# Head groups of a decode attention kernel in a hardware loop, with four fixed cache slots

## The chip, the cores and the metric

One core of one Trainium2 chip runs the kernel. The metric is the device time of one execution in microseconds, as the median of several runs. A second figure, the span, comes from the hardware profile of one run: from the first to the last instruction.

The profile names the engines: PE does matmuls and PEld loads their weights, DVE is the vector engine, ACT the scalar engine, POOL the one called GpSimd, and SP (SPq for its sequencer) is SyncE, which here issues the large DMA transfers. The granted clock is PE's clock as a share of full speed. A semaphore is a counter by which one engine waits for another. PSUM is the memory that matmuls write to.

## The reference

One decode step for two sequences (B = 2): attention with 32 query heads on 8 key/value heads over a cache of 32768 positions, a small MLP beside it, and a gate.

```python
def reference(A_x, A_k_cache, A_v_cache, A_wq, A_wo, B_x, B_w1, B_w2, B_w3, B_w4):
    xn = layernorm(A_x)                                   # [2, 1, 512]
    q  = (xn @ wq)                                        # 32 heads of 128
    p  = softmax(q @ k_cache^T * 128 ** -0.5)             # k, v: [2, 8, 32768, 128]
    s  = (p @ v_cache) @ wo
    # S is 1, so the shifted mix of the MLP's first half is zero and x1 = xn
    g  = silu(xn + gelu(layernorm(xn) @ w3) @ w4)
    return A_x + s * g
```

The caches are 268 MB in bfloat16. Everything else is 12 MB.

## The kernel before

There are 16 head groups (b, g), each with two tiles of K and two of V, 4 MB apiece. All 32 (K, V) pairs are written out by Python. Five slots of 4 MB rotate among the weights, the K tiles and the V tiles. SyncE issues all large loads in the order of the program. The code is shortened.

```python
    for r in range(NR):                       # emit_k: 8 blocks of one K tile
        nc.vector.transpose(T, kt[block r])   # DVE
        4 x nc.tensor.matmul(sc, lhsT=z[...], rhs=T[...])
    nc.scalar.activation(ep, sc, Exp, accum_out=rs)
    nc.vector.transpose(pt, ep)
    ...                                       # emit_v: sums of rs, then
    32 x nc.tensor.matmul(o, lhsT=pt[...], rhs=vt[...])     # four column tiles
    # after the second V tile of a group: ob <- o, oT, divide by the sum, onx
    ...
    for n in range(NW + 1):                   # 32 pairs, written out
        if n + 2 < NW: k_tiles[n + 2] = load_cache(A_k_cache, ...)
        if 0 < n + 1 < NW: v_tiles[n + 1] = load_cache(A_v_cache, ...)
        if n == NW - 1: load wo in five pieces
        if n < NW: eps[n] = emit_k(n)
        if n == 1: emit_mlp()                 # between two K tiles
        if n > 0: emit_v(n - 1, eps.pop(n - 1))
    for r in range(RW):                       # 32 rows x 4 column tiles: 128 matmuls
        for n in range(NQ):
            nc.tensor.matmul(s_ps[32*n:32*n+B], lhsT=oX[:, r, :], rhs=wo3[:, r, n*QW:(n+1)*QW], ...)
    # out = s_ps * g4 + x4, two DVE operations, then two small stores
```

The softmax here doesn't subtract the row's maximum and nothing guards it: scores larger than these inputs give would overflow.

## Time and profile before

| | before |
|---|---|
| time, median | 662.1 us |
| span | 660.5 us |
| bytes through SyncE's queue | 280.5 MB |
| GB/s from 100 to 640 us | 432 |
| last input byte landed | 655.3 us |
| from there to the span's end | 5.2 us |

The times of last bytes, here and below, are read from the trace's DMA packets of 1 KB and more.

From the page of the kernel before. The first line gives each engine's busy time. The rows of digits are tenths of busy time in 40 slices. The q1 row gives packets, MB and share of the 16 DMA engines. The DMA 75% row belongs to the chain of work that ended last. The last row ends with the time from issue to landing.

```profile
PE 408.5 (62%) x2590; PEld 173.7 (26%) x2622; DVE 344.9 (52%) x422; ACT 50.1 (8%) x152; POOL 6.9 (1%) x20
...
DMA  9999999999999999999999999999999999999995
...
q1 hardware_dynamic: 10232, 280.50, 98.6%
q8 instruction: 20, 0.33, 0.2%
...
DMA 75%; PE 15%; DVE 6%; issue 2%; ACT 0%; SPq 0%; DVEq 0%; ACTq 0%
...
k<-in_A_k_cache_dram SPq DMA_DIRECT2D x32, 4096.0 KB, 43.8
```

The DMA never rests. PE and DVE are far from full. A K load lands 44 us after its issue, so about 4.5 tiles of 9.7 us stand in the queue.

The windows view of the kernel before (a stretch in us, its length, busy time of PE, PEld, DVE, ACT and POOL, granted clock, DMA share, GB/s). It counts a packet in the stretch in which it starts, so a short stretch can show a share over 1.00:

```profile
20.00:22.00 2.00, 0.00 (x0) 0.00 (x0) 0.00 (x0) 1.12 (x1) 0.00 (x0) 1.00 0.65 279
22.00:26.00 4.00, 0.39 (x1) 0.11 (x2) 1.69 (x2) 0.00 (x0) 0.00 (x0) 1.00 1.17 501
...
100.00:640.00 540.00, 344.07 (x1929) 140.89 (x1960) 292.56 (x336) 37.15 (x118) 0.00 (x0) 0.77 1.00 432
```

At the end of the kernel before, the timeline shows the output matmuls in two parts. The second part waits for the last pieces of wo.

```profile
651.57 1.49 PE L402 MATMUL s_ps<-wo,oX 128*2 128x128 bf16 x64 [0.29 <-DVE oX L372]
...
654.07 2.09 PE L402 MATMUL s_ps<-wo,oX 128*2 128x128 bf16 x64 [1.01 <-DMA wo<-in_A_wo_dram]
...
656.21 0.29 DVE L410 TENSOR_TENSOR sg<-s_ps,g 98x128 f32<-98x128 f32 x1 [4.70 <-PE s_ps L402]
```

### The profile page before, as it was taken

The page shows a single profiled execution, that of the slowest core. Times are in us where ns is not written, and L with a number is a line of the kernel's source. Part 1 is how long each engine was busy: PE and PEld are TensorE (multiplying, and loading weights), DVE is VectorE, ACT ScalarE, POOL GpSimd, SP SyncE. Part 2 cuts the span into 40 slices and gives each one's busy share as a digit, 9 for nine tenths or more (in the row PEclk, how much of TensorE's full clock was granted, in tenths as well). Part 3 has the DMA queues.
Part 4 walks back from the last instruction along what each step waited for, and adds up shares of the span by engine and source line. Part 5 has one row for each costly group of instructions (what it writes and reads, how often), then busy time and mean ns, then how long its engine had stood idle before and what let it go on. Part 6 is the DMA issues. An engine that isn't in the chain of part 4 may idle for free.

```text
span 660.5 us, 6182 instructions
## 1 busy us (share of the span) xinstructions
PE 408.5 (62%) x2590; PEld 173.7 (26%) x2622; DVE 344.9 (52%) x422; ACT 50.1 (8%) x152; POOL 6.9 (1%) x20
## 2 busy tenths in 40 slices
PE   2485667565566756466776456777645776556564
PEld 2242223222222322223222122322212232222223
DVE  4563456555445655445656444565644466554450
ACT  1111100000000000000000000000000000000000
POOL 3000000000000000000000000000000000000000
PEclk9986897676888767678777777877777787767886
DMA  9999999999999999999999999999999999999995
GB/s 381 418 437 442 416 442 435 425 442 429 430 439 422 439 440 421 440 433 426 443 429 426 443 426 433 434 429 438 433 428 439 426 435 440 425 435 438 427 428 210
DMA packets 10527, 280.89 MB, mean 425 GB/s; under 512 B 1402, under 2 KB 1540, under 8 KB 1668
## 3 DMA queue, kind: packets, MB, share of 16 engines
q1 hardware_dynamic: 10232, 280.50, 98.6%
q8 instruction: 20, 0.33, 0.2%
q0 software_dynamic: 256, 0.01, 0.0%
q14 instruction: 7, 0.06, 0.0%
q10 hardware_dynamic: 12, 0.00, 0.0%
HBM read 280.50 MB, written 0.00 MB: 425 GB/s over the span
## 4 chain that ended last, share of the span: by engine, by line
DMA 75%; PE 15%; DVE 6%; issue 2%; ACT 0%; SPq 0%; DVEq 0%; ACTq 0%
DMA k<-in_A_k_cache_dram 69%; PE sc L309 11%; DMA wo<-in_A_wo_dram 6%; DVE T L301 6%; PE o L341 3%; DVE pt L320 1%; ACT ep L318 0%; PE S L337 0%; SPq L390 0%; DVE sm L336 0%; SPq L97 0%; PE s_ps L402 0%; DVE sg L410 0%; DVE out L412 0%; DVEq L301 0%
## 5 line engine op out<-in xcount | busy, mean ns | idle before, releaser
L309 PE MATMUL sc<-T,z 128*128 128x512 bf16 x992 | 295.2, 457 | 190.6 <-DVE T L301 183.3
L301 DVE STREAM_TRANSPOSE T<-k 128x1024 int32<-128x1024 int32 x256 | 292.2, 1208 | 173.4 <-DMA k<-in_A_k_cache_dram 173.4
L309 PEld LDWEIGHTS <-z 128*128 128x128 bf16 x1024 | 114.5, 112 | 370.5 <-issue 289.9
L341 PE MATMUL o<-v,pt 128*16 128x512 bf16 x1024 | 75.5, 447 | 4.9 <-DMA v<-in_A_v_cache_dram 4.9
L320 DVE STREAM_TRANSPOSE pt<-ep 128x512 bf16<-128x512 bf16 x32 | 22.8, 711 | 79.2 <-ACT ep L318 79.2
L318 ACT ACTIVATE ep<-sc 128x512 bf16<-128x512 f32 x32 | 19.1, 597 | 533.4 <-PE sc L309 533.4
L341 PEld LDWEIGHTS <-pt 128*16 128x16 bf16 x1024 | 25.6, 99 | 42.2 <-issue 25.3
L337 PE MATMUL S<-sm,ones_f 128*128 128x4 f32 x64 | 12.0, 258 | 24.8 <-DVE sm L336 24.8
L353 PE MATMUL oT<-sel_o,ob 128*128 128x4 f32 x128 | 16.9, 255 | 11.1 <-ACT ob L350 11.1
L353 PEld LDWEIGHTS oT<-sel_o,ob 128*128 128x128 f32 x128 | 15.5, 191 | 19.4 <-ACT ob L350 19.4
L337 PEld LDWEIGHTS S<-sm,ones_f 128*128 128x128 f32 x64 | 9.7, 190 | 32.6 <-DVE sm L336 32.6
L332 DVE MEMSET o<- 128x512 f32 x16 | 7.8, 485 | 13.4 <-ACT ob L350 12.3
L285 ACT COPY z<-qr 32x16 bf16<-32x16 bf16 x64 | 12.6, 197 | 11.5 <-DVE qr L232 10.8
L360 DVE TENSOR_TENSOR on<-oT,rec 128x4 f32<-128x4 f32 x16 | 2.6, 163 | 20.2 <-PE oT L353 20.2
L350 ACT COPY ob<-o 128x512 f32<-128x512 f32 x16 | 9.4, 586 | 26.2 <-PE o L341 26.2
L358 DVE RECIPROCAL rec<-S 128x4 f32<-128x4 f32 x16 | 2.9, 183 | 7.3 <-PE S L337 7.2
L318 ACT ACTIVATION_READ_ACCUMULATOR ep<-sc 128x1 f32 x32 | 6.3, 198 | 0.2
L214 PE MATMUL qT_ps<-xT,wq 128*128 128x2 bf16 x128 | 3.6, 165 | 4.5 <-DMA wq<-in_A_wq_dram 4.5
L336 DVE TENSOR_SCALAR sm<-sel_h,rs 128x4 f32<-128x4 f32 x32 | 6.1, 190 | 0.0
L214 PEld LDWEIGHTS <-wq 128*128 128x128 bf16 x128 | 3.5, 104 | 4.6 <-DMA wq<-in_A_wq_dram 4.6
L197 PE MATMUL treg<-ident,xn_bf 2*128 2x2 bf16 x4 | 0.3, 173 | 6.8 <-DVE xn_bf L189 6.8
L402 PE MATMUL s_ps<-wo,oX 128*2 128x128 bf16 x128 | 3.5, 286 | 1.3 <-DMA wo<-in_A_wo_dram 1.0
(63 smaller groups left out, 42.3 us busy)
## 6 DMA issues: line engine op xcount, KB each, us to landing
k<-in_A_k_cache_dram SPq DMA_DIRECT2D x32, 4096.0 KB, 43.8
v<-in_A_v_cache_dram SPq DMA_DIRECT2D x32, 4096.0 KB, 39.3
wq<-in_A_wq_dram SPq DMA_DIRECT2D x1, 4096.0 KB
w<-in_B_w_dram SPq DMA_DIRECT2D x2, 1792.0 KB, 37.7
wo<-in_A_wo_dram SPq DMA_DIRECT2D x1, 2048.0 KB, 34.3
wo<-in_A_wo_dram SPq DMA_DIRECT2D x1, 1536.0 KB, 37.7
wo<-in_A_wo_dram SPq DMA_DIRECT2D x1, 384.0 KB, 38.3
wo<-in_A_wo_dram SPq DMA_DIRECT2D x1, 119.0 KB
```

The lines of the kernel that those rows point to most:

```text
L214: nc.tensor.matmul(qT_ps[:, h * B:(h + 1) * B], lhsT=wq3[:, k, h * Dh:(h + 1) * Dh], rhs=xT[:, k, :], start=(k == 0), stop=(k == DK - 1),)
L285: nc.scalar.copy(out=z[32 * j:32 * j + 32, :, :, c:c + rep], in_=qr[32 * j:32 * j + 32, :, :, b, g * rep:(g + 1) * rep],)
L301: nc.vector.transpose(out=T[:, :].rearrange("p (b t k) -> p t b k", b=NB, t=RT), in_=kt[:, r * W:(r + 1) * W].rearrange("p (t b k) -> p t ...
L309: nc.tensor.matmul(sc[:, :], lhsT=z[:, nb, e, zc:zc + 128], rhs=Tb[:, nb, :, e], start=(r == 0 and nb == 0 and e == 0), stop=(r == NR - 1 ...
L318: nc.scalar.activation(out=ep[:, :], in_=sc[:, :], func=ACT.Exp, scale=inv_sqrt_dh, accum_out=rs[:, :])
L320: nc.vector.transpose(out=pt[:, :, :].rearrange("p r (t h) -> p t r h", h=rep), in_=ep[:, :].rearrange("p (t r h) -> p t r h", r=NR, h=rep),)
L332: nc.vector.memset(state["o"][:, :], 0.0)
L336: nc.vector.tensor_scalar_mul(out=sm[:, :], in0=sel_h[:, :], scalar1=rs[:, 0:1])
L337: nc.tensor.matmul(S[:, :], lhsT=ones_f[:, :], rhs=sm[:, :], start=(i == 0), stop=(i == NPART - 1))
L341: nc.tensor.matmul(o[32 * j:32 * j + VT * rep, :], lhsT=pt[:, r, a * VT * rep:(a + 1) * VT * rep], rhs=vt[:, u * VT:(u + 1) * VT, :].rearr ...
L350: nc.scalar.copy(out=ob[:, :], in_=o[:, :])
L353: nc.tensor.matmul(oT[:, :], lhsT=ob[:, t * Dh:(t + 1) * Dh], rhs=sel_o[:, t, :], start=(t == 0), stop=(t == VT - 1),)
```

## The change

The intent is a much smaller program: one head group is a turn of a hardware loop. Semaphores are not reset between turns. Instead every wait on what the loop itself counts compares with a register that grows by one turn's worth of increments. Fixed slots k0, k1, v0, v1 replace the rotation, and a fifth slot holds wo. wq first uses v0 and the MLP's weights use v1, so q and the whole MLP are done before the loop. The output stage stands in an `If` in the last turn.

```diff
-    slots = ctx.enter_context(tc.tile_pool(name="slots", bufs=SLOTS))
+    slots = ctx.enter_context(tc.tile_pool(name="slots", bufs=1))
-    wq_t = slot("wq")
+    wq_t = slot("v0", "wq")
-    k_tiles[0] = load_cache(A_k_cache, *work[0], "k0")
-    k_tiles[1] = load_cache(A_k_cache, *work[1], "k1")
-    w34 = slot("w34")
+    w34 = slot("v1", "w34")
 ...
-    v_tiles[0] = load_cache(A_v_cache, *work[0], "v0")
 ...                                  # q, then
+    emit_mlp()
 ...
-    for n in range(NW + 1):
-        ...                           # loads ahead, emit_k(n), emit_v(n - 1)
+    with tc.For_i(0, B * Hkv, 1, iteration_sync="reg_based") as n:
+        ks = [load_cache(A_k_cache, n, i, f"k{i}") for i in range(NPART)]
+        vs = [load_cache(A_v_cache, n, i, f"v{i}") for i in range(NPART)]
+        emit_z(n)
+        eps = [emit_k(k) for k in ks]
+        S = f_ps.tile([128, rep], F32, tag="S", name="S")
+        for i in range(NPART):
+            emit_v(vs[i], *eps[i], S, i)
+        emit_out(n, S)
+        with tc.If(n == B * Hkv - 1):
+            emit_end()                # loads wo, 128 output matmuls, result
```

## The prediction

> **What bounds the kernel now.** The page of the profile says 280.50 MB through the SyncE queue, the DMA row at 9 in 39 of 40 slices, and 425 GB/s over the span. The windows view gives 432 to 433 GB/s and a DMA share of 1.00 from 80 to 640 us. The Trainium skill ("DMA: Bandwidth & Descriptors", the bandwidth table at its head) puts the fabric's ceiling at 435 GB/s; this trace agrees within 1%. So about 649 us are transfer; the last wo piece lands at 655.9, and 4.6 us of tail follow. The chain of waits is 75% DMA. PE is 62% busy, DVE 52%.
>
> **What the change does.** The bytes stay the same. Five rotating slots become four fixed ones (K0, K1, V0, V1) plus one that only wo uses, so fewer loads are in flight; now a K load lands 44 us after its issue, i.e. about 4.5 tiles of 9.7 us are queued. Does the queue ever run dry?
>
> Timeline of one turn, an estimate from durations of this trace. K0 lands at T, then K1, V0, V1 at steps of 9.7 (T+9.7, T+19.4, T+29.1). Eight transposes of one K tile take 9.1 us; exp, transposition of ep and the row sum some 3.5; 32 V matmuls 1.9 to 3.5. The slots come free at about T+9 (K0), T+19 (K1), T+25 (V0; its matmuls now stand behind both K tiles) and T+31 to 33 (V1). The queue reaches their next loads at T+29, T+39, T+48.5 and T+58. So each load is issued about 20 us or more early; two to three tiles stay queued (landing falls to some 27 to 35 us). Transfers should stay back to back.
>
> Added per turn, all hidden in that slack: register arithmetic before nearly every DVE transpose, a compare at the If, a back edge, and a wait of SyncE, in the turns without the output stage, until this turn's K0 and K1 have landed (T+9.7; K0 frees then anyway). The Trainium skill ("Runtime: NRT & Kernel Launch", Instruction fetch mechanics) says a taken branch out of the fetched pages stalls for a fetch; no trace here shows its size. Over some 6 us on DVE would delay the next K0's transposes; over 15 us per turn would empty the queue.
>
> Start: wq and w34 go first (19 us), then K0 and K1 without a wait, V0 after q, V1 after the MLP (about 28 us; the queue holds work to 39). No gap. End: wo is issued about when the last V1 is, and lands last as before; the tail is the same 4.6 us, plus the loop's exit (compare, drain, one more all-engine barrier, perhaps a fetch): 1 to 4 us, the only part on the critical path.
>
> **Prediction.** 664 us, range 660.5 to 671. Faster by over 2%: 1%; within 2%: 92%; slower by over 2%: 7%.
>
> **What would show it.** DMA row still 9 nearly everywhere, about 432 GB/s in mid-span windows, 38.8 us between successive K0 landings; K landing time down to 25 to 35 us; last wo piece within 2 us of 656; a longer gap from out's issue to the end. Wrong if a window shows GB/s dipping once per turn (stall at the back edge or shallow queue), if ISA instructions stretch the DVE chain from 9.1 us a tile to over 13, or wo starts after a gap.
>
> **What would make it wrong.** Branch stalls that add up along K0 to the output; engines of the DMA drifting apart so far that the shallower queue starves the fast ones; a late issue of wo.

## More of the kernel before

SyncE's DMA issues at the start, from the timeline (start, duration, line, what):

```profile
0.74 0.42 SPq L97 DMA_DIRECT2D wq<-in_A_wq_dram  x1
1.22 0.88 SPq L87 DMA_DIRECT2D k<-in_A_k_cache_dram  x2
2.14 0.61 SPq L112 DMA_DIRECT2D w<-in_B_w_dram  x1
2.79 0.49 SPq L113 DMA_DIRECT2D w<-in_B_w_dram  x1
3.33 0.50 SPq L87 DMA_DIRECT2D v<-in_A_v_cache_dram  x1
```

All five slots are asked for within 4 us.

## The result

The changed kernel takes 670.5 us median (669.95 to 672.05, four runs) against 662.1. The ratio is 1.0129, with a 95% interval of 1.0111 to 1.0146. Ratios here are the mean time of one kernel's fast runs over the mean of the other's in the same rounds, so they are not quite the ratio of the medians quoted. Where two of my kernels are compared across calls, I multiply their ratios to the kernel before by 662 us.

The page of the changed kernel, the same rows:

```profile
PE 421.3 (63%) x2622; PEld 178.4 (27%) x2622; DVE 335.3 (50%) x407; ACT 71.3 (11%) x167; POOL 6.2 (1%) x19
...
DMA  8699999999999999999999999999999999999993
...
q1 hardware_dynamic: 10232, 280.50, 97.5%
q8 instruction: 3, 0.05, 0.0%
...
v<-in_A_v_cache_dram SPq DMA_DIRECT2D x32, 4096.0 KB, 32.9
```

The DMA row has one weak slice, the second, and then stays at 9. No turn of the loop shows a dip. A V tile lands some 33 us after its issue (39.3 before), as a shorter queue would have it. The page gives no such figure for K here; in the timeline a K0 issued at 320.70 us is first transposed at 348.87, so it had landed within 28.2 us. The windows view agrees:

```profile
20.00:22.00 2.00, 1.48 (x25) 1.40 (x24) 0.42 (x3) 0.00 (x0) 0.00 (x0) 1.00 0.38 152
22.00:26.00 4.00, 1.66 (x56) 1.37 (x56) 1.33 (x7) 1.82 (x3) 0.00 (x0) 1.00 0.02 4
...
100.00:640.00 540.00, 351.84 (x1946) 141.66 (x1945) 282.95 (x321) 58.24 (x140) 0.00 (x0) 0.79 1.00 434
```

From 22 to 26 us the DMA moved nothing to speak of. From 100 us on the loop streams at 434 GB/s, a little more than before. SyncE's issues (timeline) and one row of SyncE's waits (who waited for whom: total, times, longest) give the reason:

```profile
1.66 0.50 SPq L109 DMA_DIRECT2D w<-in_B_w_dram  x1
25.67 0.96 SPq L86 DMA_DIRECT2D k<-in_A_k_cache_dram  x2
26.96 1.01 SPq L86 DMA_DIRECT2D v<-in_A_v_cache_dram  x2
```

```profile
SPq L86 <- DVEq L390: 22.1, 1, 22.1
```

Line 390 is the loop statement. SyncE came to the first K load at 3.5 us and waited 22 us for DVE's sequencer to come to the loop. The built program says why. Inside the loop, the load into k0 waits until DVE's loop semaphore has counted the eight transposes of the previous turn. In the first turn there is no previous turn. For the comparison to hold anyway, each engine adds one turn's worth to its own semaphore as it enters the loop. DVE enters only with its last operation of the MLP: in the trace it adds to that semaphore at 25.62 us, and the load goes out at 25.67. The queue had run empty at about 21.

At the end (timeline of the changed kernel):

```profile
655.06 6.24 PE L368 MATMUL s_ps<-wo,oX 128*2 128x128 bf16 x128 [0.55 <-DVE s_ps L365]
...
663.04 0.29 DVE L375 TENSOR_TENSOR sg<-s_ps,g 98x128 f32<-98x128 f32 x1 [8.03 <-remote]
```

The view can't name what DVE waited for ("remote"). The drain that follows on PE names it: it starts at 661.47 and lasts 1.52 us, so PE was done at 662.99. The first 46 matmuls still start as in the kernel before, four every 107 ns at a clock of 0.5, 27 ns apiece. From 656.2 us on they start at an even pace of 60 ns, both where the granted clock is 0.5 and where it is 1.0 (after 660.2 us). The windows view of the output matmuls alone (stretch, length, PE, DVE, clock, DMA share, GB/s; the counts include those that overlap the edge):

```profile
655.00:656.00 1.00, 0.94 (x40) 0.01 (x1) 0.50 0.92 381
656.00:658.00 2.00, 2.00 (x48) 0.00 (x0) 0.50 0.53 203
658.00:660.00 2.00, 2.00 (x37) 0.00 (x0) 0.50 0.01 4
```

For these matmuls the built programs differ in one thing. In the loop every weight load and every matmul adds to PE's semaphore (all 128 weight loads and 134 matmuls of the body, all 260 of the `If`). In the kernel before no weight load does, and 235 of 2526 matmuls do; of the 128 output matmuls only the last.

The spans differ by 7.7 us (668.16 against 660.49). They split along the time line like this:

| stretch | before | changed | difference |
|---|---|---|---|
| start to last input byte | 655.26 | 658.31 | +3.05 |
| last input byte to the first DVE operation on s_ps | 0.95 | 4.73 | +3.78 |
| from there to the end | 4.28 | 5.12 | +0.84 |

At 40 us the changed kernel is 2.91 MB behind (13.04 against 15.95), or 6.7 us at 432 GB/s. At the last byte only 3 us of that are left. So something in the loop also wins time back.

### The profile page after: what moved, and what is told of

Its sections match the earlier page's. It is cut to its first block, busy times and chain, and to the rows that moved or that the text cites. A ratio compares the mean times of both kernels' runs of the same rounds, so it can differ in the third digit from the quotient of the medians.

```text
span 668.2 us, 7898 instructions
## 1 busy us (share of the span) xinstructions
PE 421.3 (63%) x2622; PEld 178.4 (27%) x2622; DVE 335.3 (50%) x407; ACT 71.3 (11%) x167; POOL 6.2 (1%) x19
## 5 line engine op out<-in xcount | busy, mean ns | idle before, releaser
L300 PEld LDWEIGHTS <-z 128*128 128x128 bf16 x1024 | 111.9, 109 | 301.4 <-issue 218.0
L325 PE MATMUL o<-v,pt 128*16 128x512 bf16 x1024 | 80.8, 473 | 23.7 <-DMA v<-in_A_v_cache_dram 23.7
L325 PEld LDWEIGHTS <-pt 128*16 128x16 bf16 x1024 | 28.9, 102 | 65.7 <-issue 50.8
L281 ACT COPY z<-qr 32x16 bf16 x64 | 12.9, 201 | 1.4
L368 PE MATMUL s_ps<-wo,oX 128*2 128x128 bf16 x128 | 6.2, 275 | 0.6 <-DVE s_ps L365 0.6
L368 PEld LDWEIGHTS <-oX 128*2 128x2 bf16 x128 | 6.1, 93 | 1.1 <-DVE oX L363 0.8
```

The costliest lines, as they stand in the source:

```text
L281: nc.scalar.copy(out=z[32 * j:32 * j + 32, :, :, c:c + rep], in_=qr[32 * j:32 * j + 32, :, :, bass.ds(n, 1), :].rearrange("p n e o h -> p ...
L300: nc.tensor.matmul(sc[:, :], lhsT=z[:, nb, e, zc:zc + 128], rhs=Tb[:, nb, :, e], start=(r == 0 and nb == 0 and e == 0), stop=(r == NR - 1 ...
L325: nc.tensor.matmul(o[32 * j:32 * j + VT * rep, :], lhsT=pt[:, r, a * VT * rep:(a + 1) * VT * rep], rhs=vt[:, u * VT:(u + 1) * VT, :].rearr ...
L368: nc.tensor.matmul(s_ps[32 * c:32 * c + B, :], lhsT=oX[:, r, :], rhs=wo3[:, r, c * QW:(c + 1) * QW], start=(r == 0), stop=(r == RW - 1), t ...
```

## The experiments

Theory A: the loss sits at the two ends of the loop. SyncE's first load waits for DVE's entry; the output matmuls are paced by semaphore increments. Rivals: the four fixed slots or the new order cost something (B), each turn costs something (C), and for the end, only the lowered clock makes the matmuls slow.

### e1_unroll: the loop written out

```diff
-    with tc.For_i(0, B * Hkv, 1, iteration_sync="reg_based") as n:
+    for n in range(B * Hkv):
-        with tc.If(n == B * Hkv - 1):
+        if n == B * Hkv - 1:
```

> The changed kernel with its loop written out 16 times (same four slots, same order of loads and of the last stage). Theory A (the loop costs at its entry and its end: SyncE's first K load waits for DVE to enter the loop, and the last stage's matmuls each add to a semaphore): the stretch without DMA from 22 to 26 us is gone, the 128 output matmuls take about 3.5 us in place of 7.9, time 660 to 663 us. Rival B (four fixed slots or the order of loads cost): time stays near 670. Rival C (every turn of the loop costs something): time also drops, but the loss of the loop would then show as GB/s missing in every turn of the changed kernel.

Measured: 661.6 us, ratio 0.9991 (0.9974 to 1.0008). The first K load went out at 2.12 us and nothing was missing in the DMA row:

```profile
22.00:26.00 4.00, 1.66 (x56) 1.51 (x57) 1.30 (x7) 2.20 (x4) 0.00 (x0) 1.00 1.14 492
```

The last input byte landed at 654.75, and the output matmuls ran as two parts of 1.88 us. So the slots and the order cost nothing, and B is out. All of the loss belongs to the loop's form.

### e2_dve_late: more work on DVE ahead of the loop

```diff
     emit_mlp()
+    for _ in range(13):
+        nc.vector.tensor_tensor(out=g4[0:QP, :], in0=g4[0:QP, :], in1=g4[0:QP, :], op=ALU.max)
```

> 13 dependent small DVE operations (some 5 us together) stand between the MLP and the loop; SyncE has nothing to do with them. Theory A: SyncE's first K load is issued later by the same 5 us (about 30.7 us), the stretch without DMA grows by as much, and the time rises by 4 to 5 us to about 675. Rival (SyncE is late for its own branch or instruction fetch, or the loads wait for the weights): first K load still at about 25.7 us, time within 1 us of the changed kernel.

Measured: 675.4 us, ratio 1.0194, which is 4.3 us above the changed kernel's 1.0129. The first K load moved from 25.67 to 29.98 us, also by 4.3, and the stretch without a packet of input grew from 4.2 to 8.5 us. SyncE's first issue in the loop:

```profile
29.98 0.96 SPq L86 DMA_DIRECT2D k<-in_A_k_cache_dram  x2
```

The inserted work was a little shorter than my 5 us. SyncE's own program was untouched, so it is DVE's arrival that it waits for.

### e4_end_twice and e5_before_twice: the output matmuls done twice

The edit is the same in the looped kernel and in the kernel before.

```diff
-        for r in range(RW):
+        for r in [*range(RW), *range(RW)]:
```

> The 128 output matmuls are done twice inside the loop's last turn (the second pass starts anew, result right). Theory A (each weight load and each matmul adds to a semaphore, some 30 ns apiece, 60 ns a pair): time rises by 7.7 us. Rival (only the lowered clock makes them slow): they go at the pace of the kernel before under the same clock, about 26 ns a pair, and the time rises by 3.3 us.

> The same doubling in the kernel before, where these matmuls add to no semaphore. Theory A: the 128 extra matmuls cost about 26 ns each at the lowered clock, time rises by 3 to 3.5 us to about 665.5. Rival (a pair costs 60 ns in either kernel): rises by 7.7 us.

Measured: in the loop the ratio went from 1.0129 to 1.0244, or 7.6 us for 128 more pairs, 59 ns each. In the kernel before it went to 1.0032, or 2.1 us (less than expected, in part because the last of them met a clock of 1.0). The windows view of the output matmuls alone, first in the loop (e4), then in the kernel before (e5):

```profile
658.00:660.00 2.00, 2.00 (x38) 0.00 (x0) 0.52 0.04 15
660.00:664.00 4.00, 4.00 (x71) 0.00 (x0) 1.00 0.00 0
```

```profile
654.00:656.00 2.00, 2.00 (x88) 0.00 (x0) 0.50 0.07 24
```

In the loop the pace does not change when the clock doubles. Without increments over twice as many fit in the same time at half the clock. The Trainium skill ("TensorE: Matmul & The Clock Gate", The cost: per-tile semaphore tail) says that increments by successive tiles' matmuls serialize and fits 26.3 ns for each. Two increments a pair at 60 ns are 30 ns each here, so the trace agrees in kind and nearly in size.

Could the supply of instructions set the pace instead, since a pair is also two instructions? The traces speak against it. The first matmuls run ahead at 27 ns, and PE starts the last one 2.0 us before DVE may go on (661.08 and 663.04), so what lags behind is not the matmuls. From the first output matmul to the DVE operation that waits for the last, it takes 15.61 us with 512 increments (e4), 7.98 with 256 (the changed kernel, and e8 below) and 4.19 with 128 (e9 below): 30 ns for each increment and some 0.3 us. No run takes the increments out inside the loop; e1, where they go with the loop, is the nearest.

### e6_fill: other bytes in the empty stretch

```diff
+    nc.sync.dma_start(out=wo3[:, 0:RW // 2, :], in_=wos[:, 0:RW // 2, :])   # before the loop
 ...                                   # wo's definitions move up with it
-        for a, e in wo_parts:
+        for a, e in wo_parts[1:]:
```

> The first half of wo (2 MB, 4.9 us of transfer) is loaded before the loop, so the queue has work while SyncE waits. Theory A, with its second half: the end is set by the last V1 tile and the chain after it (its matmuls, oT, the 128 output matmuls at 60 ns), not by the last byte; bytes moved from behind V1 to before K0 leave V1 where it was. So the stretch without DMA nearly goes, the last input byte lands some 4 us earlier (about 654.5), and the time does not change: 669 to 672 us. Rival (the stretch without DMA alone is the loss): the time falls by 4 us or more, to 666.

Measured: 670.6 us, ratio 1.0128: unchanged. The stretch was filled:

```profile
22.00:26.00 4.00, 1.66 (x56) 1.38 (x56) 1.33 (x7) 1.82 (x3) 0.00 (x0) 1.00 0.93 397
```

The last input byte came at 653.65, 4.7 us sooner. But the first matmul on the last V1 tile started at 649.1 us (648.9 in the changed kernel), and everything after it was as before. In the changed kernel the end hangs on the last V1 tile and the chain behind it, not on the last byte. Bytes moved from after V1 to before K0 leave V1 where it was.

### e7_end64: half as many output matmuls

They are 256 columns wide, with even and odd rows in separate column tiles, so that two more DVE operations are needed at the end. The MLP's second matmul changes with them, because it shares the layout.

```diff
-    NQ = 4
+    NQ = 2
 ...
-                    s_ps[32 * c:32 * c + B, :],
+                    s_ps[64 * (r % 2) + 32 * c:64 * (r % 2) + 32 * c + B, :],
 ...
+        nc.vector.tensor_copy(out=sg[64:QE, :], in_=s_ps[64:QE, :])
+        nc.vector.tensor_tensor(out=sg[0:QP, :], in0=s_ps[0:QP, :], in1=sg[64:QE, :], op=ALU.add)
```

> The output projection in 64 matmuls of 256 columns in place of 128 of 128 (even and odd rows apart, added by two more DVE operations); the loop's start is untouched. Theory A (each pair of weight load and matmul costs 60 ns there): 3.8 us in place of 7.7, less 0.8 us for the added operations: time falls by 3 us to about 667.5. Rival (columns or the clock set the pace): no change, 670.5 to 671.5.

Measured: 669.0 us, ratio 1.0109, so 1.3 us less in place of 3. PE was done at 660.1 in place of 663.0. That is 2.9 us, of the 3.8 that half the pairs should save:

```profile
655.12 1.87 PE L369 MATMUL s_ps<-wo,oX 128*2 128x256 bf16 x32 [0.69 <-DVE s_ps L366]
657.84 1.88 PE L369 MATMUL s_ps<-wo,oX 128*2 128x256 bf16 x32 [0.85 <-DMA wo<-in_A_wo_dram]
```

The second half now waited for wo, which took most of the rest. The wider matmuls themselves start four every 213 ns at a clock of 0.5, 53 ns each. That is twice the 27 ns of 128 columns and under the 60 ns of two increments, so e7 shows that fewer pairs of as many columns in all take less time, but not the 60 ns. The four wider DVE operations took 1.9 us where two took 0.7, and the wider layout made DVE reach the loop 1.5 us later (first K load at 27.19). The saving missed what I expected because the wait for wo was not foreseen and my cost for the added work was too low.

### e8_dve_early: DVE enters the loop early

The MLP's elementwise operations move from DVE to ACT (those that read PSUM) and GpSimd.

```diff
-        nc.vector.tensor_copy(out=hf[:, :], in_=hT[:, :])
+        nc.scalar.copy(out=hf[:, :], in_=hT[:, :])
-        nc.vector.tensor_mul(out=x2[:, :], in0=hf[:, :], in1=hf[:, :])
+        nc.gpsimd.tensor_mul(out=x2[:, :], in0=hf[:, :], in1=hf[:, :])
 ...                                   # the other six alike; one of them needs an extra copy on ACT
-        h2 = pro_ps.tile([128, QW], F32, tag="pro")
+        h2 = pro_ps.tile([128, QW], F32, tag="h2")
```

> The MLP's elementwise work goes from DVE to ACT and GpSimd (its second PSUM tile gets a bank of its own), so DVE enters the loop right after q, at about 18 us. Theory A: SyncE's first K load goes out at 18 to 19 us, before the queue is empty at 20.7; no stretch without DMA; the last V1 tile and the end come 5 to 6 us earlier: 664 to 666 us. Rival (SyncE waits for something else of the loop's entry, PE or ACT): first K load still after 25 us, time near 670.

Measured: 663.9 us, ratio 1.0021 (1.0005 to 1.0038), which is 7.2 us below the changed kernel. SyncE's issues:

```profile
1.66 0.43 SPq L109 DMA_DIRECT2D w<-in_B_w_dram  x1
17.72 0.96 SPq L86 DMA_DIRECT2D k<-in_A_k_cache_dram  x2
```

The first matmul on the last V1 tile came at 642.5, 6.4 us sooner. The loop's entry alone was thus worth most of the loss, and no other engine's entry held SyncE's first load. The first V load did wait 6.2 us for PE to enter (it went out at 25.14 us), which cost nothing while two K tiles stood in the queue.

### e9_early_end64: both

> Both of the two before. Theory A: the two costs add up, 661 to 663 us, as fast as the loop written out, leaving only the loop's exit (about 1 us). If a cost per turn existed beside them, it would stay above 665.

Measured: 662.0 us, ratio 0.9992 (0.9975 to 1.0009). A looped kernel with both repairs is as fast as the one before and as the loop written out. Of the 9.1 us between the changed kernel and e9, DVE's early entry brought 7.2 and the shorter end 1.9. That leaves little room for a cost per turn: what the loop's faster DMA gives back (about 2 us, or 0.1 us a turn) and the shorter end, which the written-out loop was not given, could still hide a small one. No window shows it. e9 beats neither kernel clearly.

### e10_early_by8: why the loop streams faster

From 100 to 640 us the kernels without a loop moved 431.8 GB/s and e8 433.1 (bytes of SyncE's packets over 540 us). Their last bytes came at 654.7 to 655.3, e8's at 651.96. The instruction queue q8 moved 20 packets of 16 KB in the former and 3 in the latter. e10 is e8 with eight groups written out in each of two turns.

```diff
-    with tc.For_i(0, B * Hkv, 1, iteration_sync="reg_based") as n:
+    with tc.For_i(0, B * Hkv, 8, iteration_sync="reg_based") as n8:
+        for j in range(8):
+            n = n8 + j
```

> e8 with eight head groups written out in each of two turns: the same start, the same last stage in the loop, but nearly as many instructions to fetch as a kernel without a loop (the profile's instruction queue moved 20 packets of 16 KB in the straight kernels, 3 in the looped ones). Straight kernels moved the input at 431.8 GB/s between 100 and 640 us, e8 at 433.1, and e8's last input byte came 2.8 us earlier. Theory D (the instruction packets take the DMA engines' time): about 18 instruction packets, last input byte back at about 654.5, time 666 to 667 us. Rival (the looped form itself, not the fetches): last input byte at about 652, time as e8, 664 us.

Measured: 673.4 us, ratio 1.0163, some 7 us over what theory D asked. The page shows

```profile
q8 instruction: 23, 0.38, 0.2%
```

and the rate fell back to 431.7 GB/s, as theory D said. But the last input byte came at 658.0, not at 654.5. The DMA did not stop at once: it moved 235 GB/s from 650 to 654 us and 48 from 654 to 658, where e8 was done. So the instruction packets go with the lower rate and a ragged end in every kernel measured. That they are the whole cause is not shown: e10's last input byte came 3.3 us after e1's with about as many packets, and why is open. The rest of e10's time lies elsewhere: the first matmul on the last V1 tile started 6.2 us later than in e8 (648.71), the chain after it ran at a clock of 0.5 and took 2.2 us longer, and the time was 4.2 to 4.4 us over the span in all four runs, where the kernel before has 1.8. The last of these no run explains. The trace as kept does not tell which DMA engine served which packet.

## Why the prediction was right or wrong

The time fell inside the range (660.5 to 671.0, measured 670.5), but near its upper edge, 6.5 us above the 664 that I named. That it fell inside is luck. The upper part of the range was left for stalls in every turn, which did not come, and two costs that I had ruled out filled it. Point by point:

- "What bounds the kernel": right. The DMA is the limit before, in the middle of the loop (434 GB/s) and in every experiment. The Trainium skill's fabric ceiling of 435 GB/s ("DMA: Bandwidth & Descriptors", the table at its head) fits all of them.
- "Each load is issued about 20 us or more early", "all hidden in that slack": right, as far as the runs tell. First transposes of successive turns stand 38.7 us apart (310.14, 348.87, 387.58 in the timeline), the landing time fell to about 33 us for V and at most 28.2 for K0, so that K0's load was issued some 18 us early, and no turn shows a dip. e1 and e9 leave little room for a cost per turn.
- "Start: K0 and K1 without a wait ... No gap": wrong. K0 has no data to wait for, but its wait names DVE's loop semaphore, and that is fed only when DVE enters the loop. I had the wait before me in the built program and took it for satisfied in the first turn. The load went out at 25.67 us in place of about 2, and the DMA stood still for 4.2 us. e2 and e8 show it from both sides: 4.3 us later for 4.3 us of added work, 7.2 us less time when DVE came at 18 us.
- "The tail is the same 4.6 us": wrong. I took the matmuls' pace from the kernel before. In the loop every weight load and matmul increments a semaphore, and 128 pairs take 7.7 us at 60 ns. From the first output matmul to the DVE operation on the result it took 7.98 us in place of 4.64, and from the last byte to that operation 4.73 in place of 0.95. e6 adds that the last byte no longer sets the end.
- "The loop's exit: 1 to 4 us, the only part on the critical path": the end after the first DVE operation on the result grew by 0.84 us, just under that. The claim that it was the only part was wrong.
- Not foreseen, and in the loop's favour: a slightly higher DMA rate and a less ragged end, which together gave back 3.6 of the 6.7 us lost by 40 us. By 640 us the loss was 4.6, so the rate gave back about 2.

## What to carry to other kernels

A wait of a register-compared loop is not free in the first turn: it holds until the engine it names has entered the loop, so ask which engine arrives last and what sits in the DMA queue until then. In this loop every weight load and every matmul carried a semaphore increment of some 30 ns. The 32 matmuls of 512 columns on a V tile hid it (1.90 us in both kernels); a burst of short ones on the critical path did not. Filling an idle stretch of the bottleneck only helps if it moves the piece that the end waits for.

## What the Trainium skill lacked or had wrong

- No page tells of loops with register-compared semaphores: that each engine's semaphore is credited when that engine enters. Here it held the first load for 22.1 us. ("Runtime: NRT & Kernel Launch" would be the place.)
- "TensorE: Matmul & The Clock Gate", The cost: per-tile semaphore tail: 26.3 ns for each increment is given for matmuls. With an increment on weight loads as well a pair took 60 ns, at granted clocks of 0.5 and 1.0 alike, and the page does not say that the pace is independent of the clock.
- "Runtime: NRT & Kernel Launch", Instruction fetch mechanics: the instruction memory is called a FIFO with purely sequential prefetch, and a stall is told of for branches out of the fetched pages alone. It does not say what a loop that fits costs. The one-group loop fetched 3 packets of 16 KB on q8, the last at 67 us, so most of its 16 turns ran without a fetch on that queue. The same section calls crossing a boundary "mostly hidden" and tells of no cost to other transfers; kernels with 20 such packets streamed at 431.8 GB/s against 433.1 (cause likely, not settled).
- "DMA: Bandwidth & Descriptors", Where 436 GB/s comes from: its warning says that about 358 GB/s bind for transfers between HBM and SBUF, though it also notes 425 GB/s for a 16 MB load. With this one core running, HBM was read at 432 to 434 GB/s for 540 us, so here the 358 did not bind.
